# Attention and a spectral feed-forward block on one core: an early table load, two sets of norms for the first pair of heads, and two output tiles that are turned inside the core

## The chip, the core and the metric

The kernel runs on one of the eight cores of a Trainium2 chip. A core has five engines, each with its own instruction stream that runs in order: PE (TensorE, matrix products and transposes), DVE (VectorE), ACT (ScalarE), POOL (GpSimd) and SP (SyncE), which here issues all transfers. Transfers run on 16 DMA engines that all of SP's transfers share. The metric is device time in microseconds of one execution; the kernel before has a median of 2169.73 us over three runs.

## The reference, cut to what matters

```
def rmsnorm(x, g):
    return x / sqrt(mean(x*x, axis=-1) + 1e-6) * g
scores = matmul(rmsnorm(q, g_q), rmsnorm(k, g_k).T) / sqrt(64)
attn = softmax(scores)
x = matmul(attn, v)                      # 8 batches, 12 heads, 448 tokens, 64 each
x = x with heads side by side            # (8, 448, 768)
u = x + real(fft(fft(x, axis=tokens), axis=features))
un = (u - mean(u)) / sqrt(var(u) + 1e-6)
out = u + relu(un @ w_ch1) @ w_ch2       # 768 -> 3072 -> 768
```

All in float32. The two weight matrices come as float64 and are converted inside the kernel.

## The kernel before, in words

Each batch goes through attention, the transform and the feed-forward block. Attention works on pairs of heads, six per batch. For a pair, `load_pair` brings q and k into a tile `raw` (112 partitions; 512 numbers of q and 512 of k on each) and v; `norm_pair` squares them, sums the squares on DVE into `ss` (16 numbers per partition: 8 of q, 8 of k), takes the power -1/2 on POOL and multiplies into `qkn`; PE transposes that (`qk`), ACT and DVE split it into a high and a low part (`QT` of the queries, `KD` and `rounded` of the keys), and then come scores `S`, row minima `mn`, exponentials `P`, transposes `pt` and the product with v. For the first two batches the squares are taken by ACT, later by POOL.

Precision is kept by splitting each operand of the large products in two parts, so every product is made of three passes. A batch's feed-forward block (`ffn`) has 24 steps `up(m)` (18 matmuls each into `h`, line L910 of the profile) and six groups of six steps `down(g, d)` (12 matmuls each into `o`, L931), in the order four `up`, six `down`. The result of `down` is added by DVE to `acc`, which lies transposed: 128 features on partitions, 448 tokens along the row, six such blocks d. Weights come through two streams of three buffers each: one transfer of 768 KB for each `up`, one of 512 KB for each `down`. The transfer for a buffer can be issued when PE has used what it held, so the `w` that step d of `down` uses is asked for when step d-3 has ended.

The 448 tokens of a batch are held in four tiles of 113, 112, 111 and 112 rows. Tiles 0 and 1 hold the even and the odd tokens of the first half *in falling order*, tiles 2 and 3 those of the second half in rising order. `token_tile` makes `u` for a tile, stores it in a DRAM buffer `u_dram` to be used later as the residual, and computes 1/std (`rstd`, the power on POOL). The output of a tile (`output_half`) loads the residual `ur` back, transposes `acc` by PE (`oT`), and DVE forms `ur = oT * rstd + ur`. `store` then writes it out. For tiles 0 and 1, whose rows run backwards, it writes the tile to `u_dram` and issues a second transfer from DRAM to DRAM that reads the rows in reverse, in pieces of 48 numbers (24 where half the columns are stored).

Batch b's feed-forward block runs merged with the attention of batch b+1, and the output of batch b-1 is made in its first four `up` steps. The last batch (7) has no attention beside it; its output is made in two halves of 384 columns (`output_last`), the first after step d=2 and the second after step d=5 of the last group.

Two things set the order. A scheduling step places the instructions of each engine by a model of their times and by the order in which the program writes them, and gives out the buffers of a tag in the order in which the program asks for them; tag `P` has eight buffers, used by `P`, `u`, `un`, `ur` and others. After that each engine, and SP with its transfers, runs strictly in that order: a transfer that waits holds up all that stand behind it.

In the profile nearly all instructions of DVE, ACT and POOL have the line L113, that of a helper which records them, so they are told apart by their tiles.

Of the kernel before, what the change touches and what calls it, by code (L numbers as in the profile page):

```python
# [22 lines left out]
C = 112  # L23
# [66 lines left out]
def spectral_block(ctx, tc, q, k, v, g_q, g_k, w1, w2, d1, d2, out, nb=B):  # L90
# [74 lines left out]
    def add(o, a, b_):  # L165
        V.tensor_tensor(out=o, in0=a, in1=b_, op=ALU.add)
# [18 lines left out]
    u_dram = dram.tile([2, 4, N1, DM], F32, name="u_dram")  # L185
# [679 lines left out]
    residual = {}  # L865

    def output_half(b, i, half, tag):
        n, t0 = LENS[i], OFFS[i]
        if half == 0:
            residual[i] = slot("P", f"ur{b}_{i}")[:, :DM]  # L870
            for r in rows_of(n):
                nc.sync.dma_start(residual[i][r], u_dram[b % 2, i, r])
        u = residual[i]
        op = bank(tag, f"oT{b}_{i}_{half}")
        for j in range(3):
            nc.tensor.transpose(  # L876
                op[:n, j * 128 : (j + 1) * 128],
                accs[b][:, 3 * half + j, t0 : t0 + n],
                ident,
            )  # L880
# [16 lines left out]
    def ffn(b, unT):  # L897
# [27 lines left out]
        def down(g, d):  # L925
# [47 lines left out]

    load_gains()
# [16 lines left out]
    for b in range(nb):  # L991
        merge(
# [25 lines left out]
```

## Time and profile before

| | |
|---|---|
| runs (us) | 2169.73, 2168.72, 2171.92 |
| profiled execution, its own time | 2168.48 us |
| its span, first to last instruction | 2166.7 us |
| PE busy | 2082.8 us, 96% of the span |
| DVE, ACT, POOL busy | 1556.7, 1055.5, 342.6 us |
| mean granted clock of PE | 0.983 |
| moved by DMA | 424.74 MB, mean 196 GB/s |

A row of the timeline gives the start and the length in us, the engine, the line, the operation, the tiles it writes and reads, and in brackets how long the engine was idle ahead of it and what released it. `SPq` is the issue of a transfer on SP. A row of the windows gives a stretch, then for each engine its busy time and (x) its number of instructions, the granted clock of PE, the busy share of the 16 DMA engines and GB/s. Rows of transfers give their number, their size and the median time from issue to landing, where the trace has it.

### The profile page before, as it was taken

The numbers are of one execution on the slowest core, as the hardware profiler recorded it, in microseconds if no ns is written. First come the engines' busy times: TensorE is split into PE (matmuls) and PEld (weight loads), VectorE is DVE, ScalarE is ACT, GpSimd is POOL, SyncE is SP. The second block draws the span as 40 slices with busy tenths as digits, with TensorE's granted clock in tenths as the row PEclk, the third lists the DMA queues.
The fourth block names the chain that finished last, engine by engine and source line by source line (L and its number), as shares of the span: only waits on it lengthen the run. The fifth ranks groups of instructions, "written<-read, shape, count | busy, mean of one in ns | idle before, by whom it ended". The sixth has DMA issues, their size and how long they took to land.

```text
span 2166.7 us, 31325 instructions
## 1 busy us (share of the span) xinstructions
PE 2082.8 (96%) x11224; PEld 1857.7 (86%) x11224; DVE 1556.7 (72%) x3003; ACT 1055.5 (49%) x2258; POOL 342.6 (16%) x196
## 2 busy tenths in 40 slices
PE   7877999899999999999999999999999999999997
PEld 4556777789999999999999999999999999998997
DVE  7888878978785788758786688857787588753122
ACT  7967866455552555435552455425553455422100
POOL 3324434221110111001110111101110011000000
PEclk8988999999999999999999999999999999999999
DMA  5647777677565855667565765658556675449665
GB/s 167 185 131 266 243 262 243 204 236 224 162 174 184 244 173 165 186 200 218 165 174 178 224 194 172 179 183 241 166 173 190 188 219 165 157 157 287 214 211 138
DMA packets 298301, 424.74 MB, mean 196 GB/s; under 512 B 186609, under 2 KB 224482, under 8 KB 298146
## 3 DMA queue, kind: packets, MB, share of 16 engines
q1 hardware_dynamic: 298146, 422.74, 63.8%
q8 instruction: 89, 1.46, 0.3%
q14 instruction: 66, 0.54, 0.1%
HBM read 362.50 MB, written 65.27 MB: 197 GB/s over the span
## 4 chain that ended last, share of the span: by engine, by line
PE 79%; DVE 6%; DMA 6%; ACT 4%; issue 2%; POOL 1%; SPq 0%; DVEq 0%; POOLq 0%; ACTq 0%
PE o L931 29%; PE h L910 28%; PE S L375 6%; PE av L485 4%; DMA dblw<-w 4%; PE pt L473 4%; PE y L590 2%; PE qk L327 1%; DMA w<-w 1%; ACT P L113 1%; PE oT L876 1%; POOL magw L728 1%; PE x L622 1%; DVE qkn L113 1%; PE un L822 1%
## 5 line engine op out<-in xcount | busy, mean ns | idle before, releaser
L931 PE MATMUL o<-hs,w 128*128 128x448 f32 x3456 | 794.8, 372 | 7.0 <-DMA w<-w 2.6
L910 PE MATMUL h<-unT,w 128*128 128x448 f32 x3456 | 778.7, 370 | 4.1 <-ACT unT L113 1.6
L931 PEld LDWEIGHTS o<-hs,w 128*128 128x128 f32 x3456 | 639.5, 189 | 64.5 <-DMA w<-w 4.9
L910 PEld LDWEIGHTS h<-unT,w 128*128 128x128 f32 x3456 | 639.2, 188 | 58.2 <-issue 2.4
L113 ACT ACTIVATE P<-S,mn 112x448 f32<-112x448 f32 x384 | 243.7, 636 | 197.9 <-DVE mn L113 183.9
L113 ACT ACTIVATE hs<-h 128x448 fp32r<-128x448 f32 x192 | 104.3, 543 | 311.6 <-PE h L910 309.7
L113 DVE TENSOR_REDUCE mn<-S 112x1 f32<-112x448 f32 x384 | 233.7, 618 | 28.1 <-PE S L375 25.5
L113 DVE SCALAR_TENSOR_TENSOR hs<-h,hs 128x448 fp32r<-128x448 f32 x192 | 119.4, 622 | 149.2 <-ACT hs L113 147.4
L113 DVE TENSOR_TENSOR acc<-o,acc 128x448 f32<-128x448 f32 x240 | 148.7, 620 | 96.8 <-PE o L931 94.2
L113 POOL TENSOR_TENSOR qkn<-raw 112x1024 f32<-112x1024 f32 x36 | 68.6, 1906 | 697.8 <-PE qk L327 354.8
L113 POOL TENSOR_TENSOR ss<-ss,nhalf 112x16 f32<-112x16 f32 x48 | 144.7, 3014 | 183.2 <-DVE ss L113 164.8
L375 PE MATMUL S<-KD,QT 128*112 128x448 f32 x384 | 152.3, 399 | 16.3 <-ACT KD L113 11.1
L113 ACT CAST T<-pt 128x448 fp32r<-128x448 f32 x216 | 113.1, 533 | 99.8 <-PE pt L473 98.5
L485 PE MATMUL av<-T,vhl 128*128 128x448 f32 x432 | 153.4, 383 | 0.0
L113 DVE TENSOR_TENSOR T<-pt,T 128x448 fp32r<-128x448 f32 x216 | 131.6, 618 | 26.6 <-ACT T L113 25.6
L375 PE MATMUL S<-rounded,QT 128*112 128x448 f32 x384 | 143.2, 375 | 0.4 <-DMA v<-v 0.4
L113 DVE TENSOR_SCALAR P<-P,sm 112x448 f32<-112x448 f32 x288 | 122.5, 463 | 4.1
L473 PE MATMUL pt<-ident,P 112*128 112x112 f32 x864 | 121.8, 259 | 0.0
L473 PEld LDWEIGHTS pt<-ident,P 112*128 112x128 f32 x864 | 102.6, 140 | 15.5
L728 POOL TENSOR_TENSOR magw<-magw,dblw 128x512 uint32<-128x512 uint32 (+1 forms) x46 | 75.4, 1639 | 172.9 <-DVE magw L724 103.1
L113 POOL TENSOR_TENSOR rstd<-st,nhalf 112x1 f32<-112x1 f32 (+2 forms) x32 | 19.6, 612 | 492.3 <-DVE st L113 489.2
L375 PEld LDWEIGHTS S<-KD,QT 128*112 128x112 f32 x384 | 69.2, 181 | 27.9 <-ACT KD L113 13.7
(117 smaller groups left out, 2521.9 us busy)
## 6 DMA issues: line engine op xcount, KB each, us to landing
w<-w SPq DMA_DIRECT2D x192, 768.0 KB, 4.5
w<-w SPq DMA_DIRECT2D x288, 512.0 KB, 4.3
dblw<-w SPq DMA_DIRECT2D x28, 512.0 KB, 5.1
dblw<-w SPq DMA_DIRECT2D x18, 768.0 KB, 5.9
raw<-q SPq DMA_DIRECT2D x96, 112.0 KB, 3.3
raw<-k SPq DMA_DIRECT2D x96, 112.0 KB, 3.7
v<-v SPq DMA_DIRECT2D x96, 96.0 KB, 3.1
u_dram<-u SPq DMA_DIRECT2D x24, 336.0 KB, 3.4
```

What stands on the lines that cost most here:

```text
L113: ins = emit(*args, **kwargs)
L327: nc.tensor.transpose(pt[:, c * C : (c + 1) * C], qk[:, i, c].rearrange("t h d -> t (h d)"), ident[:C, :C],)
L375: ins = nc.tensor.matmul(s_, QT[:, h, cs], K[:, h], start=step == 0, stop=step == 1)
L473: nc.tensor.transpose(pt[:, c * C : (c + 1) * C], Pc[c][:, 512 * h + j * 128 : 512 * h + (j + 1) * 128], ident[:C, :C],)
L485: nc.tensor.matmul(av[:, :S], lv, T[:, i], start=(j == 0 and i == 0), stop=False)
L590: nc.tensor.matmul(o, src[:, par, t0 : t0 + n], D1[:, ri, par, cols], start=i != 1, stop=i != 0,)
L622: nc.tensor.transpose(xp[:n, i * 128 : (i + 1) * 128], src[:, 3 * half + i], ident)
L728: behind(nc.gpsimd.tensor_tensor(out=bits, in0=bits, in1=low, op=ALU.add))
L822: nc.tensor.transpose(pt[:, OFFS[i] : OFFS[i] + LENS[i]], uns[i][:, p * 128 : (p + 1) * 128], ident[: LENS[i], : LENS[i]],)
L876: nc.tensor.transpose(op[:n, j * 128 : (j + 1) * 128], accs[b][:, 3 * half + j, t0 : t0 + n], ident,)
L910: pace(nc.tensor.matmul(o, w[:, a, c], unT[c][:, z], start=n == 0, stop=n == 17))
L931: pace(nc.tensor.matmul(o, w[:, a, f], hs[4 * g + f][:, z], start=n == 0, stop=n == 11))
```

## The change

Three edits.

1. ScalarE's function table is loaded by an instruction of its own at the very start. Before, the load stood directly ahead of ACT's first square and carried that square's waits.
2. For the first pair of the first batch the norms are computed in two passes, q and then k, each with its square, sum, scaling and power, instead of one pass over both.
3. In the last batch tiles 0 and 1 are turned ahead of the store. At the start of that batch's feed-forward block `turn_rstd` copies `rstd` of the two tiles into 32 columns, and reads it and the residual from DRAM back into DRAM in reverse row order. In the last group of `down` the sum is written by two instructions, one for the first 225 tokens in reverse order into a new tile `back` (three feature blocks in one buffer of tag `P`), one for the other 223 into `acc`. The transposes of tiles 0 and 1 read `back`, and the rows come out in rising order, so that `store` writes them to the output directly.

```
-        if b < EARLY:
-            A.activation(sq, flat, AF.Square)
...
-        V.tensor_reduce(ss, sq, axis=AX.X, op=ALU.add)
...
-        G.tensor_tensor(out=ss, in0=ss, in1=nhalf[:C], op=ALU.pow)
+        ss = sb.tile([C, 2, 8], F32, tag="ss", name=f"ss{b}_{p}")
+        for part in ((slice(0, 1), slice(1, 2)) if b + p == 0 else (slice(0, 2),)):
+            n = part.stop - part.start
+            sq = qk[:, part].rearrange("t i c h d -> t (i c h) d")
+            flat = raw[:, part].rearrange("t i h c d -> t (i h c) d")
+            if b < EARLY:
+                A.activation(sq, flat, AF.Square)
...
+            V.tensor_reduce(s_, sq, axis=AX.X, op=ALU.add)
...
+            G.tensor_tensor(out=s_, in0=s_, in1=nhalf[:C, : 8 * n], op=ALU.pow)
@@ def store
-        if i < 2:
+        if i < 2 and b == nb - 1:
+            nc.sync.dma_start(out[b, i : i + 223 : 2, cols], u[n - N2 : n, cols])
+            if i == 0:
+                nc.sync.dma_start(out[b, 224:225, cols], u[:1, cols])
+        elif i < 2:
@@ new
+    def turn_rstd(b):
+        for i in range(2):
+            n = LENS[i]
+            t = sb.tile([N1, 32], F32, tag=f"turned{i}", name=f"turned{b}_{i}", bufs=1)
+            V.tensor_copy(t[:n], rstds[b, i][:n].broadcast_to([n, 32]))
+            nc.sync.dma_start(r_dram[0, i, :n], t[:n])
+            nc.sync.dma_start(
+                r_dram[1, i, :n].rearrange("t (c d) -> c t d", c=16),
+                r_dram[0, i, n - 1 :: -1].rearrange("t (c d) -> c t d", c=16),
+            )
+            nc.sync.dma_start(
+                u_dram[2, i, :n].rearrange("t (c d) -> c t d", c=16),
+                u_dram[b % 2, i, n - 1 :: -1].rearrange("t (c d) -> c t d", c=16),
+            )
+            nc.sync.dma_start(t[:n], r_dram[1, i, :n])
+            turned_rstd[i] = t[:, :1]
@@ def output_half
+                src = u_dram[2 if turn else b % 2, i]
+                nc.sync.dma_start(residual[i][r], src[r])
...
+                back[half][:, j, NT - t0 - n : NT - t0]
+                if turn
+                else accs[b][:, 3 * half + j, t0 : t0 + n],
@@ def down
+            elif b == nb - 1 and g == NG - 1:
+                if d % 3 == 0:
+                    back.append(
+                        slot("P", f"back{d}")[:, : 3 * NT].rearrange(
+                            "r (d t) -> r d t", d=3
+                        )
+                    )
+                add(back[-1][:, d % 3], o[:, NT - 1 :: -1], acc[:, d, NT - 1 :: -1])
+                add(acc[:, d, NT:], o[:, NT:], acc[:, d, NT:])
@@ start
+    nc.scalar.preload_act_table(AF.Exp)
     load_gains()
@@ for b in range(nb)
+        if b == nb - 1:
+            turn_rstd(b)
```

What the scheduling step makes of it, at the places that the prediction speaks of. In these rows the first word is the line, `waits` names the engines and the eight counters of transfers (DMAHW0 to 7) that the instruction waits for.

The start, SP's first transfers, before and then with the change:

```order
L225 DMA raw_0_113<-q 112x4x64 x2
L225 DMA raw_0_113<-k 112x4x64 x2
L190 DMA gains<-g_q 64x1 x2
L190 DMA gains<-g_k 64x1 x2
L225 DMA raw_1_144<-q 112x4x64 [waits DMAHW0_49]
```

```order
L226 DMA raw_0_115<-q 112x4x64 x2
L191 DMA gains<-g_q 64x1 x2
L191 DMA gains<-g_k 64x1 x2
L226 DMA raw_0_115<-k 112x4x64 x2
L226 DMA raw_1_150<-q 112x4x64 [waits DMAHW0_49]
```

The keys' two loads moved behind the four of the gains. And DVE's first instructions there, before and then with the change (`ss` the sums of squares):

```order
L969 MEMSET warm 128x512
L113 TENSOR_REDUCE ss_0_138<-qkn_0_136 112x16 [waits Activation_49]
L113 SCALAR_TENSOR_TENSOR gains<-gains 128x1 [waits DMAHW6_49,DMAHW7_49,DMAHW5_49,DMAHW4_49]
L113 TENSOR_SCALAR ss_0_138<-ss_0_138 112x16 [waits DVE_49]
L113 TENSOR_TENSOR qkn_0_136<-raw_0_113,ss_0_138 112x2x4x64 [waits DMAHW1_49,DMAHW0_49,Pool_49]
L113 TENSOR_TENSOR qkn_0_136<-raw_0_113,ss_0_138 112x2x4x64 [waits DMAHW3_49,DMAHW2_49]
```

```order
L1010 MEMSET warm 128x512
L113 TENSOR_REDUCE ss_0_139<-qkn_0_138 112x8 [waits Activation_49]
L113 TENSOR_SCALAR ss_0_139<-ss_0_139 112x8 [waits DVE_49]
L113 SCALAR_TENSOR_TENSOR gains<-gains 128x1 [waits DMAHW4_49,DMAHW5_49,DMAHW3_49,DMAHW2_49]
L113 TENSOR_TENSOR qkn_0_138<-raw_0_115,ss_0_139 112x2x4x64 [waits DMAHW1_49,DMAHW0_49,Pool_49]
L113 TENSOR_REDUCE ss_0_139<-qkn_0_138 112x8 [waits Activation_49]
L113 TENSOR_SCALAR ss_0_139<-ss_0_139 112x8 [waits DVE_49]
L113 TENSOR_TENSOR qkn_0_138<-raw_0_115,ss_0_139 112x2x4x64 [waits DMAHW7_49,DMAHW6_49,Pool_49]
```

The keys' sum stands behind the queries' product, which waits for POOL. From there to the middle of the first batch's feed-forward block many neighbouring instructions of all engines change places; from the second batch's feed-forward block to the last group of the last batch PE's order is the same.

The border between the feed-forward blocks of batch 6 and batch 7, SP's transfers, before (`u_1`, `u_3` are tiles of batch 7, `ur` residuals of batch 6; `w_249` to `w_251` are for steps d=3 to d=5 of batch 6's last group):

```order
L770 DMA w_170_19821<-w_2_80 128x1536 [waits DMAHW6_49,PE_49]
L635 DMA u_dram<-u_1_19645 112x768 [waits DMAHW7_49,DVE_49]
L770 DMA w_249_19837<-w_5_107 128x1024 [waits DMAHW0_49,PE_49]
L770 DMA w_250_19853<-w_5_107 128x1024 [waits DMAHW1_49,PE_49]
L635 DMA u_dram<-u_3_19667 112x768 [waits DMAHW2_49,DVE_49]
L872 DMA ur_0_19968<-u_dram 112x768 [waits DMAHW3_49,Activation_49]
L872 DMA ur_0_19968<-u_dram 1x768 [waits DMAHW4_49]
L872 DMA ur_1_20008<-u_dram 112x768 [waits DMAHW5_49,Activation_49]
L872 DMA ur_2_20046<-u_dram 96x768 [waits DMAHW6_49]
L770 DMA w_251_19869<-w_5_107 128x1024 [waits DMAHW7_49,PE_49]
```

With the change (the row behind the last is the load of `w_251`):

```order
L883 DMA r_dram<-r_dram 16x113x2 [waits DMAHW6_49]
L773 DMA w_170_19827<-w_2_81 128x1536 [waits PE_49]
L891 DMA turned_0_19925<-r_dram 113x32 [waits DMAHW2_49,DMAHW0_49]
L638 DMA u_dram<-u_1_19651 112x768 [waits DMAHW3_49,DVE_49]
L773 DMA w_249_19843<-w_5_108 128x1024 [waits DMAHW4_49,PE_49]
L887 DMA u_dram<-u_dram 16x112x48 [waits DMAHW5_49,DMAHW3_49]
L773 DMA w_250_19859<-w_5_108 128x1024 [waits PE_49]
L638 DMA u_dram<-u_3_19673 112x768 [waits DMAHW7_49,DVE_49]
L882 DMA r_dram<-turned_1_19931 112x32 [waits DVE_49]
L901 DMA ur_0_19986<-u_dram 112x768 [waits DMAHW1_49,Activation_49]
L901 DMA ur_0_19986<-u_dram 1x768 [waits DMAHW2_49]
L901 DMA ur_1_20026<-u_dram 112x768 [waits Activation_49]
```

The reversing transfers and the waits for their landings stand between the loads of the weights; a first reversing copy and the store of `turned_0` stand ahead of this piece.

The residuals of batch 7 (`ur_0_21124` to `ur_3_21154`) are loaded before the change right behind the border:

```order
L770 DMA w_252_19885<-w_0_102 128x1024 [waits DMAHW2_49,PE_49]
L770 DMA w_253_19901<-w_0_102 128x1024 [waits DMAHW3_49,PE_49]
L872 DMA ur_0_21124<-u_dram 112x768 [waits DMAHW4_49,PE_49]
L872 DMA ur_1_21135<-u_dram 112x768 [waits DMAHW5_49,PE_49]
L872 DMA ur_2_21144<-u_dram 96x768 [waits DMAHW6_49]
L872 DMA ur_0_21124<-u_dram 1x768 [waits DMAHW7_49]
L872 DMA ur_3_21154<-u_dram 112x768 [waits DMAHW0_49,PE_49]
L872 DMA ur_2_21144<-u_dram 15x768 [waits DMAHW1_49]
L770 DMA w_254_19917<-w_0_102 128x1024 [waits DMAHW2_49,PE_49]
```

With the change they are loaded in the last group (`w_284` to `w_287` are the weights of its steps d=2 to d=5):

```order
L773 DMA w_284_21026<-w_5_108 128x1024 [waits DMAHW7_49,DMAHW4_49,PE_49]
L773 DMA w_285_21110<-w_5_108 128x1024 [waits DMAHW5_49,DMAHW0_49,PE_49]
L901 DMA ur_0_21146<-u_dram 112x768 [waits DMAHW1_49]
L901 DMA ur_1_21156<-u_dram 112x768
L901 DMA ur_2_21164<-u_dram 96x768
L901 DMA ur_3_21174<-u_dram 112x768
L773 DMA w_286_21127<-w_5_108 128x1024 [waits DMAHW6_49,PE_49]
L901 DMA ur_0_21146<-u_dram 1x768
L901 DMA ur_2_21164<-u_dram 15x768 [waits DMAHW7_49]
L773 DMA w_287_21144<-w_5_108 128x1024 [waits DMAHW0_49,PE_49]
L855 DMA out_dram<-ur_0_21146 112x384 [waits DMAHW6_49,DMAHW1_49,DVE_49]
L857 DMA out_dram<-ur_0_21146 1x384 [waits DMAHW2_49]
```

All four residuals, 1344 KB, now stand between the weights of d=3 and of d=4: the program asks for a buffer of tag `P` for `back` ahead of those for the residuals, so these are given out behind it.

More of the change, by code (lines that the diff above doesn't have):

```diff
@@ L184, in spectral_block @@
     D2 = rounded[:N1, 2 * S :].rearrange("s (i c a t) -> s i c a t", i=2, c=2, a=2)
-    u_dram = dram.tile([2, 4, N1, DM], F32, name="u_dram")
+    u_dram = dram.tile([3, 4, N1, DM], F32, name="u_dram")
+    r_dram = dram.tile([2, 2, N1, 32], F32, name="r_dram")
     def load_gains():
@@ L249, in norm_pair @@
         qk = sb.tile([C, 2, NC, 2, D], F32, tag="qk", name=f"qkn{b}_{p}", bufs=1)
-        sq = qk.rearrange("t i c h d -> t (i c h) d")
-        flat = raw.rearrange("t i h c d -> t (i h c) d")
-        nth = b * NPAIR + p
-        if b < EARLY:
-            A.activation(sq, flat, AF.Square)
-        else:
-            G.tensor_tensor(out=sq, in0=flat, in1=flat, op=ALU.mult)
-        ss = sb.tile([C, 16], F32, tag="ss", name=f"ss{b}_{p}")
-        V.tensor_reduce(ss, sq, axis=AX.X, op=ALU.add)
-        V.tensor_scalar(
-            out=ss, in0=ss, scalar1=1.0 / D, scalar2=EPS, op0=ALU.mult, op1=ALU.add
-        )
-        G.tensor_tensor(out=ss, in0=ss, in1=nhalf[:C], op=ALU.pow)
+        ss = sb.tile([C, 2, 8], F32, tag="ss", name=f"ss{b}_{p}")
[5 more added lines that the diff above has]
+                A.activation(sq, flat, AF.Square)
+            else:
+                G.tensor_tensor(out=sq, in0=flat, in1=flat, op=ALU.mult)
+            s_ = ss[:, part].rearrange("t i n -> t (i n)")
+            V.tensor_reduce(s_, sq, axis=AX.X, op=ALU.add)
+            V.tensor_scalar(
+                out=s_, in0=s_, scalar1=1.0 / D, scalar2=EPS, op0=ALU.mult, op1=ALU.add
+            )
+            G.tensor_tensor(out=s_, in0=s_, in1=nhalf[:C, : 8 * n], op=ALU.pow)
         for i in range(2):
@@ L266, in norm_pair @@
                 in0=raw[:, i],
-                in1=ss[:, 8 * i : 8 * i + 8]
+                in1=ss[:, i]
                 .rearrange("t (h c) -> t h c", h=2)[:, :, :, None]
@@ L865, in spectral_block @@
     residual = {}
+    turned_rstd = {}
+    back = []
+    def turn_rstd(b):
[14 more added lines that the diff above has]
+            turned_rstd[i] = t[:, :1]
     def output_half(b, i, half, tag):
         n, t0 = LENS[i], OFFS[i]
+        turn = i < 2 and b == nb - 1
         if half == 0:
@@ L871, in output_half @@
             for r in rows_of(n):
-                nc.sync.dma_start(residual[i][r], u_dram[b % 2, i, r])
+                src = u_dram[2 if turn else b % 2, i]
+                nc.sync.dma_start(residual[i][r], src[r])
         u = residual[i]
@@ L882, in output_half @@
         V.scalar_tensor_tensor(
-            out=uh, in0=op[:n, :384], scalar=rstds[b, i][:n], in1=uh,
+            out=uh, in0=op[:n, :384],
+            scalar=(turned_rstd[i] if turn else rstds[b, i])[:n], in1=uh,
             op0=ALU.mult, op1=ALU.add,
```

2 lines of the change are left out of this document (1 added, 1 removed).

## The prediction

> **What bounds the kernel now.** I read the page first (span, busy shares, PE's slices), then a table by stage, then the timeline at the two ends and at the last border between batches, because the change acts only there.
>
> ```profile
> span 2166.7 us, 31325 instructions
> PE 2082.8 (96%) x11224; PEld 1857.7 (86%) x11224; DVE 1556.7 (72%) x3003; ACT 1055.5 (49%) x2258; POOL 342.6 (16%) x196
> PE   7877999899999999999999999999999999999997
> ```
>
> The slices show a kernel that PE bounds from the fifth slice (some 220 us) to the fortieth. Work hidden there costs nothing; what remains is the start, where PE has gaps, and the last slice.
>
> The table by stage (stretch, its length, then PE, PE's weight loads, DVE, ACT, POOL, granted clock, DMA share, GB/s):
>
> ```profile
> 20.00:60.00 40.00, 31.66 (x142) 22.41 (x141) 34.75 (x63) 38.18 (x89) 16.50 (x8) 0.85 0.62 190
> 140.00:180.00 40.00, 25.51 (x120) 21.49 (x121) 31.41 (x63) 24.00 (x48) 10.01 (x7) 0.67 0.36 120
> 1944.00:1954.00 10.00, 10.00 (x56) 9.23 (x55) 5.91 (x17) 5.32 (x11) 1.11 (x2) 1.00 0.65 227
> 1954.00:1964.00 10.00, 10.00 (x61) 9.24 (x60) 3.01 (x9) 3.45 (x5) 0.54 (x1) 1.00 0.81 236
> 1964.00:1974.00 10.00, 8.00 (x46) 7.21 (x45) 5.64 (x11) 2.96 (x8) 0.55 (x1) 1.00 1.03 274
> 1974.00:1984.00 10.00, 10.00 (x56) 9.22 (x56) 3.44 (x6) 1.09 (x2) 0.00 (x0) 1.00 1.03 324
> 2130.00:2140.00 10.00, 10.00 (x51) 9.28 (x50) 2.50 (x4) 1.16 (x3) 0.00 (x0) 1.00 0.01 2
> ```
>
> From 20 to 60 us ACT is the full engine (38.18 of 40), from 140 to 180 none is: a chain of waits bounds there. At 1964 the transfers fill the DMA engines and PE loses 2 us; at 2130 they are idle.
>
> **The start (edits 1 and 2).**
>
> ```profile
> 1.70 1.02 SPq L225 DMA_DIRECT2D raw<-k  x2
> 2.77 1.20 SPq L190 DMA_DIRECT2D gains<-g_q  x2
> 4.01 1.25 SPq L190 DMA_DIRECT2D gains<-g_k  x2
> 5.05 1.28 ACT L113 ACT_TABLE_LOAD   x1 [5.05 <-DMA raw<-k]
> 6.34 1.06 ACT L113 ACTIVATE qkn<-raw 112x1024 f32<-112x1024 f32 x1
> 7.43 1.22 DVE L113 TENSOR_REDUCE ss<-qkn 112x16 f32<-112x1024 f32 x1 [6.04 <-ACT qkn L113]
> 8.69 0.17 DVE L113 TENSOR_SCALAR ss<-ss 112x16 f32<-112x16 f32 x1
> 9.02 2.92 POOL L113 TENSOR_TENSOR ss<-ss,nhalf 112x16 f32<-112x16 f32 x1 [6.91 <-DVE ss L113]
> 11.98 1.29 DVE L113 TENSOR_TENSOR qkn<-raw,ss 112x512 f32<-112x512 f32 x2 [3.11 <-POOL ss L113]
> 12.81 1.11 PE L327 MATMUL qk<-ident,qkn 112*128 112x112 f32 x8 [2.11 <-DVE qkn L113]
> 14.52 0.63 ACT L113 ACTIVATE KD<-qk,gains 64x448 fp32r<-64x448 f32 x1
> 16.73 0.72 PE L375 MATMUL S<-KD,QT 128*112 128x448 f32 x1 [2.80 <-ACT KD L113]
> ...
> L113 POOL TENSOR_TENSOR rstd<-st,nhalf 112x1 f32<-112x1 f32 (+2 forms) x32 | 19.6, 612 | 492.3 <-DVE st L113 489.2 <-DMA ur<-u_dram 3.1
> ```
>
> The first scores (16.73) wait for the first `KD` (14.52). The table load waited for k and took 1.28; it now runs while nothing is there. Keys landed at 5.0, 2.3 after their last issue ended (2.72), so queries land near 4.0 (issue ended 1.66). Then the square of half the size 0.65, the sum 0.65, the scaling 0.3 with its gaps: POOL can start at 5.65. No row has a power of 8 columns; those of 1 (0.61) and 16 (2.92) are its bounds, and on the line between them lies 1.7, which I take: 7.4, the queries' product to 8.05. The keys, behind the gains' 2.45 us of issues, land at 7.5; square to 8.15, sum (DVE free at 8.05) to 8.85, scaling to 9.1, power to 10.85, product 11.55, PE 0.75: `KD` at 12.3 instead of 14.52, 2.2 earlier. ACT, which is full afterwards, gets one instruction more (0.2): **-2.0**. With powers of 2.92 twice the keys come to 14.5 and the gain is 0; with 0.61 it is 3.4. The keys' later load costs nothing, since DVE is held by the queries' product until 8.05; without that cover it would cost 2.45.
>
> Behind this the scheduling step swaps neighbours for some 400 us. The work is the same and ACT stays full, so I take 0; with the idle 14.5 of 40 us in the row of 140 to 180 in mind I allow 3 us either way.
>
> **The border of batch 6 and 7.**
>
> ```profile
> 1953.72 0.32 SPq L635 DMA_DIRECT2D u_dram<-u  x1
> 1955.22 3.11 SPq L770 DMA_DIRECT2D w<-w  x2
> 1961.15 0.34 SPq L770 DMA_DIRECT2D w<-w  x1
> 1969.50 2.72 PE L931 MATMUL o<-hs,w 128*128 128x448 f32 x12 [2.00 <-DMA w<-w]
> ...
> u_dram<-u SPq DMA_DIRECT2D x24, 336.0 KB, 3.4
> u_dram<-u SPq DMA_DIRECT2D x8, 288.0 KB, 2.9
> out_dram<-ur SPq DMA_DIRECT2D x7, 288.0 KB, 6.0
> w<-w SPq DMA_DIRECT2D x288, 512.0 KB, 4.3
> ```
>
> Here the weights come just in time: the last of the group, issued at 1961.15, was used at 1969.50 after a stall of 2.00. The change adds two reversing copies of 336 KB, two reversals of `rstd` in pieces of two numbers, and four small transfers, and SP waits for landings in between. The store of `u_1` (1953.72) now stands behind two such waits, for which I take 2; the weights of d=4 (second issue of the pair at 1955.22, ending 1958.33) then wait for that store's landing (3.4): issue at 1953.7 + 2 + 3.4 + 0.6 = 1959.7 instead of 1958.0. A reversing copy ahead of a transfer cost up to 3.1 (288 KB stored behind one: 6.0 against 2.9), and moves its 336 KB in no less than 1.1 at the 324 GB/s of the full stretch from 1974. I take 2 each. Landing near 1965 against a need at 1964.0, the step is about 1 late; of what reaches the last weights one residual load (288 KB) has moved behind. **+1.3**. Below, 0: the 10 us to 1964 have 1.9 us of unused DMA (share 0.81), the 10 ahead of them 3.5 (0.65). Above, 7: two copies at 3.1 and two reversals that cost the same by piece are 12.4, less these 5.4. ACT's square of `u_3` waits for its store and gets 2 later, with `unT` behind it; the stall at 1969 covers that. DVE's two copies of `rstd` (0.2 each) lie in stretches where DVE is busy 3 to 6 of 10 us. The residuals that no longer load behind 1967 free the engines where PE waited for nothing: no gain.
>
> The Trainium skill, page "DMA: Bandwidth & Descriptors", section Specifications, speaks against this edit: below 512 B a DMA engine reads, modifies and writes. Pieces here have 192 B and 8 B; by that rule the second rival below is the likelier case. No row here prices an 8 B piece.
>
> **The end.**
>
> ```profile
> 2139.24 0.32 SPq L770 DMA_DIRECT2D w<-w  x1
> 2141.68 0.32 SPq L770 DMA_DIRECT2D w<-w  x1
> 2147.59 5.12 PE L931 MATMUL o<-hs,w 128*128 128x448 f32 x24
> 2152.74 0.62 DVE L113 TENSOR_TENSOR acc<-o,acc 128x448 f32<-128x448 f32 x1 [1.81 <-PE o L931]
> 2153.82 2.19 DVE L113 SCALAR_TENSOR_TENSOR ur<-oT,rstd,ur 113x384 f32<-113x384 f32 x4 [0.46 <-PE oT L876]
> 2158.41 0.56 SPq L854 DMA_DIRECT2D out_dram<-u_dram  x1
> 2160.44 1.31 SPq L863 DMA_DIRECT2D out_dram<-ur  x1
> ...
> SPq L1012 <- DMA out_dram<-ur: 3.9, 1, 3.9
> ...
> u_dram<-ur SPq DMA_DIRECT2D x4, 168.0 KB, 2.9
> ```
>
> PE's last product ends at 2152.71, the span at 2166.7: a tail of 14.0, of which DVE needs 3.3 (to 2156.01). The rest is SP: it waits for the writes to `u_dram`, reverses, issues the last store at 2160.44 to 2161.75, and waits 3.9 for it (2165.65); 1.05 follow. With the change: two sums (0.62 splits into about 0.4 and 0.4), transposes behind the first, DVE's four sums start 0.85 behind the product and end at 3.05. Three stores are left to issue, the last starting at 3.9; it lands 2.9 later (6.8), and with 1.05 the tail is 7.85: **-6.15**. A reversed read from PSUM is in no row; at twice the price it adds 0.25.
>
> Against it stand the residuals, now behind the weights of d=3 (2139.24, landing 4.3 later at 2143.5) and ahead of those of d=4. 1344 KB at 274 to 324 GB/s are 4.2 to 5.0, and the 512 KB of d=4 another 1.6 to 1.9: landing at 2149.3 to 2150.4, where PE needs them at 2147.6. The nearest row agrees: at the border a weight behind three such loads and a store came 8.3 after its issue (1961.15 to 1969.50); 2141.68 + 8.3 = 2150.0. Stall **+2.4**; 0 if the idle engines of 2130 to 2140 take it faster, 3.7 with another residual's 1.3 on top. DVE's sums of the first half wait for the last rows of the residuals; d=4 on PE covers them.
>
> Sum: 2168.48 - 2.0 + 1.3 - 6.15 + 2.4 = 2164.0. The execution lies 1.25 under the median of 2169.73 and 0.24 under the fastest run, so I put half of that back: **2164.6**.
>
> **Rivals.**
>
> *The residuals come in time.* For it: DMA share 0.01 before. Against it: the 8.3 above. 2164.6 - 2.4 = 2162.2, chance 0.20.
>
> *The reversals hold SP and the DMA engines at the border (the other side).* Place: between the weights of steps d=3 to d=5 of batch 6; price up to 7; from 5.1 more than my 1.3 nothing of the gain is left. For it: the stall that is there already and share 1.03; against: 5.4 us of free DMA ahead of it, and PE's need at d=4 was met with time. At 7: 2170.3. Chance 0.12.
>
> *The start gives nothing*: two powers of 2.92, or the swapped order loses what the early norms won. 2166.6 to 2169, chance 0.23. By the Trainium skill, "TensorE: Matmul & The Clock Gate", Part 1, an idle window of about 3.4 us halves PE's clock; the clock of 0.67 in the row of 140 to 180 agrees that this stretch has such windows. By it each one more would cost up to 1.7, an estimate from the page's figure, on top of this case.
>
> **How the numbers follow.** The forecast has 0.45. Range 2157.5 to 2170.3: below, the residuals in time, a start of -3.4 and a lucky order; above, the border's 7. A measurement of this kernel tells about 0.2% (4.3 us, below 2165.4) from no change. The forecast is 0.8 inside that, so two thirds of it count as faster (0.30), with all of the first rival (0.20) and little of the third: 0.52. Slower (above 2174.1) needs the border's 7 and a bad order: 0.08. The same: 0.40.
>
> **What would show it.** Right: `KD` first at about 12.3; PE stalled 2 to 3 us on `w` ahead of d=4 of the last group, and 3 to 4 at the border; 8 us from PE's last product of d=5 to the end. Wrong: a tail above 10 us, a stall on `w` at the border above 6, a power of 8 columns near 2.9, or a first score 2 us earlier whose lead is gone by 220 us.

## The result: slower, by 0.68%

| | before | with the change |
|---|---|---|
| median (us) | 2169.25 (four runs) | 2184.03 (four runs, 2182.99 to 2186.51) |
| ratio, 95% interval | | 1.0068 (1.0056 to 1.0081) |
| profiled execution, its time and span | 2168.48, 2166.7 | 2184.48, 2182.6 |

The forecast was 2164.6, 19.4 us below. The milestones of PE in the two traces say where the 15.9 us between the two spans lie:

| stretch (us) | before | change | |
|---|---|---|---|
| start to the first product of batch 1's feed-forward block | 478.5 | 488.2 | +9.7 |
| from there to the first product of batch 6's | 1244.8 | 1245.1 | +0.3 |
| from there to the first product of batch 7's | 249.0 | 258.0 | +9.0 |
| from there to the start of the last product | 180.0 | 183.9 | +3.9 |
| from there to the end | 14.4 | 7.4 | -7.0 |

**The start.** The timeline of the changed kernel, the rows that answer to those of before:

```profile
0.73 1.28 ACT L1015 ACT_TABLE_LOAD   x1 [0.73 <-PEq L1045]
2.15 9.98 PE L1013 MATMUL warmed<-warm,ident 128*128 128x512 f32 x16 [2.15 <-POOL ident masks.py:199]
5.59 1.67 POOL L113 TENSOR_TENSOR ss<-ss,nhalf 112x8 f32<-112x8 f32 x1 [3.49 <-DVE ss L113]
7.29 0.69 DVE L113 TENSOR_TENSOR qkn<-raw,ss 112x512 f32<-112x512 f32 x1 [1.10 <-POOL ss L113]
10.82 0.69 DVE L113 TENSOR_TENSOR qkn<-raw,ss 112x512 f32<-112x512 f32 x1 [1.76 <-POOL ss L113]
11.97 0.93 PE L330 MATMUL qk<-ident,qkn 112*128 112x112 f32 x8
12.56 1.07 ACT L113 CAST QT<-qk 64x448 fp32r<-64x448 f32 x2 [4.43 <-PE qk L330]
13.65 0.63 ACT L113 ACTIVATE KD<-qk,gains 64x448 fp32r<-64x448 f32 x1
15.86 0.46 PE L378 MATMUL S<-KD,QT 128*112 128x448 f32 x1 [2.96 <-ACT KD L113]
```

The power of 8 columns took 1.67, and the keys' product ended at 11.51. But the queries, ready at 7.98, were not transposed until 11.97: the warming products stand ahead of them in PE's order and run to 12.13. So the casts of the queries (12.56) still stand ahead of `KD` on ACT, and the first score comes 0.87 earlier (15.86 against 16.73), not 2.2.

That lead is gone by 40 us: ACT's 24th exponential `P` ends at 39.4 against 38.7 before, its 32nd at 48.2 against 44.8, and PE's 96th product `S` at 120.7 against 111.8. So nearly the whole 9.7 us of the start are lost between 30 and 120 us, and in several waits. One of them, in the timeline of the changed kernel:

```profile
58.84 2.79 SPq L204 DMA_DIRECT2D d2s<-d  x2
65.37 0.57 ACT L113 CAST rounded<-d2s 113x452 fp32r<-113x452 f32 x1 [2.11 <-DMA d2s<-d]
68.43 0.52 ACT L113 COPY T<-pt 128x448 f32<-128x448 f32 x1
69.01 1.55 PE L452 MATMUL av<-T,v 128*128 128x448 f32 x2 [4.29 <-ACT T L113]
```

ACT stands for 2.11 until the transform's table `d2s` has landed, converts it, does four other things, and PE waits 4.29 for the copy `T` behind them. Before, the table's load was issued at 57.08, 1.76 earlier, and ACT did not wait for it. By stretches (length, PE, PE's weight loads, DVE, ACT, POOL, clock, DMA share, GB/s), the changed kernel:

```profile
20.00:60.00 40.00, 29.23 (x127) 18.96 (x128) 34.47 (x59) 35.65 (x82) 15.69 (x8) 0.83 0.55 164
1974.00:1984.00 10.00, 8.28 (x29) 6.85 (x29) 3.22 (x11) 4.14 (x9) 1.08 (x2) 0.66 0.94 255
1984.00:1994.00 10.00, 8.02 (x38) 7.16 (x38) 4.23 (x8) 1.34 (x3) 0.00 (x0) 0.83 0.79 169
```

From 20 to 60 ACT is no longer full: 35.65 of 40 against 38.18. From 60 to 120 it is busy for 52.25, against 58.55 before. That makes 8.8 us of ACT's time lost in 100 us, of the 9.7.

**The border of batch 6 and 7.** SP's issues and PE's long waits in the timeline of the changed kernel, then two rows of SP's waits (in total, times, longest; the longest are those at the border):

```profile
1961.04 0.58 SPq L883 DMA_DIRECT2D r_dram<-r_dram  x1
1961.84 1.72 SPq L773 DMA_DIRECT2D w<-w  x1
1968.64 0.24 SPq L891 DMA_DIRECT2D turned<-r_dram  x1
1968.98 0.87 SPq L638 DMA_DIRECT2D u_dram<-u  x1
1969.94 0.85 SPq L773 DMA_DIRECT2D w<-w  x1
1975.21 4.82 PE L963 MATMUL o<-hs,w 128*128 128x448 f32 x12 [3.76 <-DMA w<-w]
1986.94 4.26 PE L963 MATMUL o<-hs,w 128*128 128x448 f32 x12 [1.98 <-DMA w<-w]
```

```profile
SPq L891 <- DMA r_dram<-r_dram: 7.8, 2, 5.0
SPq L883 <- DMA r_dram<-turned: 2.4, 2, 2.2
```

The reversal of 14 KB of `rstd`, issued at 1961.04, had landed when SP went on at 1968.64, 7.6 later. The store of `u_1` went out at 1968.98 instead of 1953.72 (10.0 of these 15.3 us are the lag with which batch 6 began), the weights behind it at 1969.94, and PE stood for weights at 1975.21, and again at 1986.94. With these two stops its granted clock fell: 0.66 and 0.83 in the stretches from 1974 and from 1984, where before it was 1.00. At full speed the same work would have taken 3.4 and 1.7 us less, as an estimate from these two rows. So the border's 9.0 are about half waiting (the waits for weights sum to 6.1, with a third one of 0.37, against 2.00 before) and about half the lower clock behind them (5.1). What the DMA engines did meanwhile, in 40 slices of 0.5 us from 1956 to 1976 (busy tenths, then GB/s):

```profile
DMA  9999688998997982104548972679999785644039
GB/s 250 224 246 295 240 277 336 315 318 289 436 344 271 147 106 39 1 1 27 38 38 86 74 74 37 135 270 418 345 296 330 203 158 231 256 180 172 25 55 235
```

From 1963.5 to 1968.5 (slices 16 to 25) 1 to 86 GB/s moved. The reversing copy of the residual, in nearly as many pieces but of 192 B, does nothing of the kind in the same trace. The first row below is the stretch behind the first such copy (issued at 1953.55), the second lies behind the reversal of `rstd`, and the third is the landing of the second such copy (issued at 1973.91):

```profile
1957.00:1961.00 4.00, 4.00 (x22) 3.69 (x21) 2.13 (x3) 1.97 (x4) 0.00 (x0) 1.00 0.91 289
1964.00:1968.00 4.00, 4.00 (x25) 3.71 (x24) 2.20 (x7) 0.94 (x1) 0.02 (x1) 1.00 0.54 42
```

```profile
u_dram<-u_dram SPq DMA_DIRECT2D x1, 336.0 KB, 4.4
```

So 1792 pieces of 192 B land in 4.4, and 1808 of 8 B in 7.6. The number of pieces is not what makes the difference.

**The end**, from the timeline and SP's waits of the changed kernel:

```profile
2170.35 2.69 PE L963 MATMUL o<-hs,w 128*128 128x448 f32 x12 [2.20 <-DMA w<-w]
2175.62 0.39 DVE L113 TENSOR_TENSOR back<-o,acc 128x225 f32<-128x225 f32 x1 [1.86 <-PE o L963]
2175.93 0.38 DVE L113 TENSOR_TENSOR acc<-o,acc 128x223 f32<-128x223 f32 x1
2178.72 1.30 SPq L870 DMA_DIRECT2D out_dram<-ur  x3
```

```profile
SPq L1056 <- DMA out_dram<-ur: 1.4, 1, 1.4
```

The stall at d=4 is there (2.20), the reversed sums cost 0.39 and 0.38, the last three stores are issued at 2178.72, SP waits 1.4 for them, and 7.0 us pass between the end of PE's last product (2175.6) and the end, where it was 14.0.

### The profile page after: what moved, and what is told of

Its sections match the earlier page's. It is cut to its first block, busy times and chain, and to the rows that moved or that the text cites. A ratio compares the mean times of both kernels' runs of the same rounds, so it can differ in the third digit from the quotient of the medians.

```text
span 2182.6 us, 31336 instructions
## 1 busy us (share of the span) xinstructions
PE 2090.8 (96%) x11224; PEld 1860.2 (85%) x11224; DVE 1552.0 (71%) x3013; ACT 1056.0 (48%) x2259; POOL 342.4 (16%) x197
## 4 chain that ended last, share of the span: by engine, by line
PE 78%; DMA 7%; ACT 6%; DVE 5%; POOL 2%; issue 2%; SPq 1%; POOLq 0%; DVEq 0%; ACTq 0%
PE h L942 29%; PE o L963 28%; PE S L378 6%; PE av L488 4%; PE pt L476 4%; DMA dblw<-w 3%; DMA w<-w 2%; PE y L593 1%; PE qk L330 1%; ACT P L113 1%; POOL magw L731 1%; PE oT L905 1%; PE x L625 1%; DVE eo L113 1%; PE av L493 1%
## 5 line engine op out<-in xcount | busy, mean ns | idle before, releaser
L963 PE MATMUL o<-hs,w 128*128 128x448 f32 x3456 | 798.1, 373 | 18.1 <-DMA w<-w 10.8
L113 DVE TENSOR_TENSOR acc<-o,acc 128x448 f32<-128x448 f32 (+1 forms) x240 | 147.2, 614 | 86.6 <-PE o L963 83.7
L113 POOL TENSOR_TENSOR ss<-ss,nhalf 112x16 f32<-112x16 f32 (+1 forms) x49 | 143.5, 2929 | 195.9 <-DVE ss L113 165.3
L378 PE MATMUL S<-KD,QT 128*112 128x448 f32 x384 | 152.3, 398 | 12.1 <-ACT KD L113 7.3
```

What stands on the lines that cost most here:

```text
L113: ins = emit(*args, **kwargs)
L378: ins = nc.tensor.matmul(s_, QT[:, h, cs], K[:, h], start=step == 0, stop=step == 1)
L963: pace(nc.tensor.matmul(o, w[:, a, f], hs[4 * g + f][:, z], start=n == 0, stop=n == 11))
```

## The experiments

Two theories at the outset. *Order and pieces*: the 9.7 us come from the order in which the scheduling step puts the neighbours after edit 2, and the 9.0 from the reversal of `rstd` in pieces of 8 B. The rivals: the table load or the two passes themselves cost the start; SP's chain of waits costs the border, whatever the pieces; the edits influence each other. The kernel before, run beside these, had medians of 2168.3 to 2169.9 and single runs from 2164.4 to 2175.1, and a profiled execution lay up to 9 us beside its kernel's median; so ratios with their intervals decide. The last four columns are the milestones of each kernel's profile, the stretches of the table above without the second.

| kernel | median | ratio (95%) | batch 1 starts | 6 to 7 | in 7 | tail |
|---|---|---|---|---|---|---|
| edit 1 alone | 2168.3 | 0.9993 (0.9983 to 1.0003) | 475.5 | 249.0 | 179.1 | 14.4 |
| edit 2 alone | 2177.86 | 1.0042 (1.0026 to 1.0057) | 486.8 | 251.5 | 179.5 | 14.5 |
| edit 2, old order | 2170.53 | 1.0010 (0.9999 to 1.0020) | 477.0 | 251.2 | 180.4 | 14.6 |
| no edit, new order | 2180.54 | 1.0053 (1.0034 to 1.0071) | 489.1 | 251.6 | 179.9 | 14.1 |
| edit 2, old order of loads | 2179.56 | 1.0039 (1.0029 to 1.0050) | 483.7 | 250.9 | 179.8 | 14.1 |
| edit 3 alone | 2178.09 | 1.0039 (1.0024 to 1.0053) | 480.3 | 259.6 | 185.8 | 7.4 |
| edit 3, wide pieces | 2169.05 | 0.9996 (0.9983 to 1.0008) | 476.9 | 253.2 | 189.2 | 7.3 |
| whole change, wide pieces | 2176.56 | 1.0038 (1.0025 to 1.0051) | 488.1 | 253.0 | 184.1 | 7.5 |
| edit 3, turned late | 2174.72 | 1.0031 (1.0019 to 1.0043) | 480.0 | 252.7 | 195.1 | 7.5 |
| the same, residuals early | 2177.1 | 1.0038 (1.0026 to 1.0050) | 483.0 | 253.2 | 189.0 | 7.6 |
| the same with edit 1 | 2178.19 | 1.0040 (1.0028 to 1.0053) | 478.1 | 253.1 | 191.6 | 7.6 |
| the same, wide pieces | 2169.02 | 0.9990 (0.9981 to 0.9999) | 476.5 | 252.4 | 185.4 | 7.5 |
| turned at the border, wide, residuals early, edit 1 | 2166.42 | 0.9983 (0.9973 to 0.9994) | 477.9 | 251.7 | 182.9 | 7.6 |
| the same, residuals spread | 2169.19 | 1.0003 (0.9991 to 1.0016) | 477.6 | 252.2 | 184.4 | 7.6 |

### The start: which edit, and is it the work or the order

Edit 1 alone is one line:

```
+    nc.scalar.preload_act_table(AF.Exp)
     load_gains()
```

> Edit 1 alone: the function table loaded at the start, everything else as before (every engine's order is then the same as before). In the changed kernel the first 480 us cost 9.9 us more than before. Theory (order): that loss belongs to the new order that edit 2 sets off, so this kernel stays within 1.5 us of the kernel before (2167.7 to 2170.7), with a first score some 1 us earlier at most, because POOL's power of 16 columns (2.92) still stands behind the landing of the keys. Rival (table): the early load itself disturbs the start, and about 10 us are lost here: 2179.

Measured 0.9993: the early table costs nothing that could be told and gives at most 0.17%. In its timeline the first score comes at

```profile
15.69 0.46 PE L375 MATMUL S<-KD,QT 128*112 128x448 f32 x1 [2.81 <-ACT KD L113]
```

1.04 earlier, with POOL's power of 16 columns left as it was. (In all kernels with edit 1, edit 2 or both the first score comes between 15.24 and 15.96; the two do not add up.) Edit 2 alone (`norm_pair` of the change in the kernel before):

> Edit 2 alone: the first pair's norms in two passes, q and then k, and with it the new order of neighbours up to the middle of the first batch's feed-forward block; no early table load, no edit 3. Theory (order): the whole loss of the first 480 us is here, 2179 +- 2, with batch 1's feed-forward block starting near 488 instead of 478.5. Rival (table): the two passes are harmless and this kernel is at 2167 to 2170.

Measured 1.0042, 8.0 us, with batch 1 at 486.8. Its timeline has the stop at 65 us too:

```profile
64.36 0.57 ACT L113 CAST rounded<-d2s 113x452 fp32r<-113x452 f32 x1 [1.66 <-DMA d2s<-d]
67.99 1.86 PE L451 MATMUL av<-T,v 128*128 128x448 f32 x2 [3.82 <-ACT T L113]
```

Then the same edit with the order held. The table `ISSUE` lists, for each engine, the instructions in the order of the kernel before:

```
+    for engine, text in ISSUE.items():
+        ...
+        for one, two in zip(rows, rows[1:]):
+            tc.add_manual_dep(mine[two], mine[one].name,
+                DependencyInfo(NoSync, DATA), reason="issue order")
```

> Edit 2 alone, with the order of every engine behind the first pair's norms held to that of the kernel before (PE's first 1793 instructions, DVE's 642, ACT's 556, SP's 300, POOL's 90), so that only the two passes themselves and the first loads differ. Theory (order): the loss is gone, 2166 to 2170. Rival (work): the two passes themselves, with one ACT instruction, two DVE and one POOL instruction more, cost it, and this kernel stands beside edit 2 alone at 2177 to 2181.

Measured 1.0010 (0.2 us faster to 4.3 slower): with the old order 7.3 of the 8.0 us are gone. The reverse, the kernel before with the new order and not one instruction changed:

> None of the three edits: the kernel before, its instructions unchanged, with the order of every engine held to the one that edit 2 sets off (PE's first 1793 instructions, DVE's 642, ACT's 556, SP's 300, POOL's 90). Theory (order): it loses what edit 2 alone lost, 8 +- 2: 2177.5. Rival (the loss needs the two passes together with the new order): within 2 us of the kernel before.

Measured 1.0053, 12 us, more than the 8 +- 2 expected; but its interval overlaps that of edit 2 alone, so the two cannot be told apart. Nothing but the order of the first quarter was new, and the stop at 66 us is in its timeline as well:

```profile
66.41 0.57 ACT L211 CAST rounded<-d2s 113x452 fp32r<-113x452 f32 x1 [2.00 <-DMA d2s<-d]
70.04 1.31 PE L547 MATMUL av<-T,v 128*128 128x448 f32 x2 [4.17 <-ACT T L211]
```

ACT's time tells which kernels lose and where. Two rows of the stretches, the kernel before and then its instructions in the new order, and the waits of ACT from 20 to 120 us in the same two (in total, times, longest; one row of before, three of the other):

```profile
60.00:120.00 60.00, 49.82 (x255) 32.31 (x254) 55.21 (x95) 58.55 (x129) 24.38 (x14) 1.00 0.54 152
60.00:120.00 60.00, 48.94 (x224) 32.40 (x224) 48.06 (x87) 53.05 (x119) 20.52 (x10) 0.91 0.55 165
```

```profile
ACT P L113 <- DVE mn L113: 0.6, 2, 0.5
ACT P L211 <- DVE mn L211: 4.8, 8, 2.0
ACT rounded L211 <- DMA d2s<-d: 2.0, 1, 2.0
ACT w1e L827 <- POOL magw1e L826: 1.5, 1, 1.5
```

| kernel | ACT busy, 20 to 60 | 60 to 120 | idle in the 100 us | batch 1 starts |
|---|---|---|---|---|
| before | 38.18 | 58.55 | 3.3 | 478.5 |
| edit 1 alone | 38.02 | 58.52 | 3.5 | 475.5 |
| edit 2, old order | 37.70 | 58.53 | 3.8 | 477.0 |
| the whole change | 35.65 | 52.25 | 12.1 | 488.2 |
| edit 2 alone | 35.54 | 52.69 | 11.8 | 486.8 |
| no edit, new order | 35.49 | 53.05 | 11.5 | 489.1 |

The three kernels with the new order have ACT idle 8 to 9 us longer there than the kernel before, the two others do not. The waits are the same in the three: some 5 us for DVE's row minima `mn` in eight waits, 1.7 to 2.1 for the table `d2s`, 2.1 for two steps of POOL on the weights. So the order is the cause, shown from both sides, and it costs through many small waits of ACT. Is one of them, the late load of the table, most of it? In the next kernel only SP's order is held:

```
+        if engine not in ('SP',):
+            continue
```

> Edit 2 alone, with only SP's first 300 transfers held to the order of the kernel before; the other engines are ordered by the scheduling step as it likes. In the changed kernel ACT waits 2.11 us at 65 us for the transform's table, whose load stands later in SP's order, and PE 4.29 behind it. Theory (one late load): with the transfers in the old order most of the loss is gone, 2170 to 2173. Rival (the order of the engines as a whole): no single load is the cause, and this kernel is still at 2175 or above; PE's and ACT's order differs from that of both other kernels here.

Measured 1.0039: the theory of the one load falls. Batch 0's feed-forward block does begin early there (175.9, against 178.5 before and 184.3 with edit 2 alone), so up to that point the order of the loads cost; but then 7.8 us are lost inside that block, where the engines' order is a third one. Between 178 and 488 us PE waits there 6.3 us for ACT's part of the weights `w` and 7.0 for ACT's copies `T`, against 1.5 and 3.4 before. That the order of SP alone does not give the time back is shown; what each single row of the order costs stays open.

### The border: pieces, or SP's chain

Edit 3 alone, with the start of before:

> Edit 3 alone: turning rstd and the residual at the border of batch 6 and 7, reversed sums and the direct stores at the end; the start as before, in the order of before. The traces of before and after give +8.8 at the border, +4 within batch 7 (2.2 of it the stall on the weights of d=4) and -7.0 behind the last product. Theory (the three edits add up): 2169.3 + 5.8 = 2175 +- 1.5. Rival (the loss at the border depends on what the new start shifts ahead of it): within 2 us of before or below.

Measured 1.0039, 8.2 us: the edits add up (0.42% and 0.39% alone, less 0.07% for edit 1, against 0.68% together, all within the intervals). Two of its stretches, in the columns of the table by stage, and the wait in its timeline:

```profile
1956.00:1960.00 4.00, 3.92 (x23) 3.44 (x21) 2.58 (x9) 0.95 (x2) 0.40 (x1) 1.00 0.80 40
1960.00:1964.00 4.00, 3.83 (x25) 3.35 (x23) 0.00 (x0) 0.00 (x0) 0.00 (x0) 1.00 0.70 54
```

```profile
1970.60 4.13 PE L961 MATMUL o<-hs,w 128*128 128x448 f32 x12 [6.76 <-DMA w<-w]
```

Behind the reversal (issued at 1955.44) the DMA engines are busy for 0.70 to 0.80 of the time and move 40 to 54 GB/s, against 324 in the full stretch of before. If SP's waiting for landings were all, it would leave them idle. But SP does wait as well: 7.4 us, from 1957.05 to 1964.47, for the landing of this reversal. The test changes the pieces alone:

```
-                r_dram[1, i, :n].rearrange("t (c d) -> c t d", c=16),
-                r_dram[0, i, n - 1 :: -1].rearrange("t (c d) -> c t d", c=16),
+                r_dram[1, i, :n].rearrange("t (c d) -> c t d", c=2),
+                r_dram[0, i, n - 1 :: -1].rearrange("t (c d) -> c t d", c=2),
```

> Edit 3 alone, with one difference: the two reversals of rstd in DRAM go in 2 x 113 pieces of 64 B instead of 16 x 113 pieces of 8 B (the same 14 KB). In the trace of edit 3 alone the moved rate falls to 33 to 45 GB/s for some 8 us right behind the issue of the first of these reversals at 1955.44, with the DMA engines busy, and PE then waits 6.76 us for weights. Theory (pieces): the number of pieces is the price; with an eighth of them the weights come through, the loss at the border (10.6 us from the start of batch 6 to that of batch 7) falls to 3 +- 3 and the time to 2171 +- 2. Rival (SP's chain): what costs is that SP waits for one landing after the other ahead of the weights, whatever the pieces; the loss stays at 8 to 11 and the time at 2176 to 2180.

Measured 0.9996: 9 us came off, with the same transfers in SP's chain, so the rival in its form "whatever the pieces" falls. From its timeline:

```profile
1952.55 0.66 SPq L881 DMA_DIRECT2D r_dram<-r_dram  x1
1955.73 0.24 SPq L889 DMA_DIRECT2D turned<-r_dram  x1
1973.00 4.26 PE L961 MATMUL o<-hs,w 128*128 128x448 f32 x12 [2.00 <-DMA w<-w]
```

The next step on SP goes 3.2 behind the issue, where it was 9.0 (1955.44 to 1964.47) with pieces of 8 B; SP's wait for the landing is 1.5 instead of 7.4. So the small pieces can cost in two ways, by holding SP and by slowing the weights that are already under way, and this pair alone does not part them. The profiled execution of the kernel with wide pieces lies 6.7 us above the median, so its columns do not show all of the gain: the border fell from 259.6 to 253.2, but batch 7 took 189.2, with a clock of 0.67 from 2004 to 2014 behind a stall of 2.93. The same in the whole change:

> The whole change with one difference: rstd is reversed in 2 x 113 pieces of 64 B instead of 16 x 113 of 8 B. The whole change has a ratio of 1.0068 (1.0056 to 1.0081) to the kernel before. Theory (pieces and order are two separate losses): the 9 us that wide pieces gave to edit 3 alone (2178.1 to 2169.05) come off here as well, 2169.5 + 14.8 - 9 = 2175 +- 2. Rival (with the new start the border is late anyway): 2180 or above.

Measured 1.0038: 6.5 us less than the whole change by the ratios (0.0030), of the 9 expected; the 1.0038 that remains is about what edit 2 alone costs (1.0042). Moving the turning away from the border is the other way to spare the weights; each step is issued behind a weight load of batch 7 and held there:

```
+    TURN = {(1, 0): (turn_a, 0), (1, 1): (turn_a, 1), (1, 4): (turn_b, 0),
+            (2, 1): (turn_b, 1), (2, 4): (turn_c, 0), (3, 1): (turn_c, 1)}
...
+                if b == nb - 1 and (g, d) in TURN:
+                    step, i = TURN[g, d]
+                    step(b, i)
                 down(g, d)
```

> Edit 3 alone, with the turning moved: the copies, reversals and loads of rstd and the reversal of the residual are issued one after the other behind weight loads of the groups 1 to 3 of batch 7's feed-forward block, where the weights are early, not at the border. Theory: the border loss is gone (batch 7 starts within 2.5 us of the kernel before), the stall at d=4 of the last group stays (2.1 to 2.2), the tail stays 7 shorter: 2169.9 - 7 + 4 = 2167 +- 2. Rival (the reversals cost wherever they stand): the loss moves with them into batch 7 as stalls on weights of 4 us or more, 2172 or above.

The rival held, at 1.0031. Its timeline, and the weights among its transfers from 2060 to 2080:

```profile
2064.45 1.11 SPq L890 DMA_DIRECT2D r_dram<-r_dram  x1
2076.77 7.67 PE L975 MATMUL o<-hs,w 128*128 128x448 f32 x24 [5.99 <-DMA w<-w]
```

```profile
w<-w SPq DMA_DIRECT2D x4, 512.0 KB, 10.8
```

In the middle of a steady group PE stops for 5.99 behind the reversal (x1, 14 KB), and weights land 10.8 behind their issue, against 4.3 over the kernel before. SP waits for no reversal here: the weights that PE stops for were issued at 2065.93, right behind it, and landed at 2076.72. So the second way costs by itself. The reversing copy of the residual was issued 0.6 us ahead of the reversal, though, so which of the two slows the weights is open up to here; the kernel with wide pieces below settles it.

### The residuals, and a version that beats both

```
+                if b == nb - 1 and g == 4 and d < 4:
+                    load_residual(b, d)
                 down(g, d)
```

> As the kernel with the turning moved, and the four residuals of batch 7 are asked for and loaded one by one behind weight loads of group 4, ahead of the buffers for the reversed sums, instead of all between the weights of d=3 and d=4 of the last group. Theory: the stall of 2.2 at d=4 goes and nothing takes its place: 2 to 3 below the kernel with the turning moved alone, 2164.5 +- 2. Rival (1344 KB cost PE the same wherever they are loaded): same time as with the turning moved alone.

The stall at d=4 is gone from the trace (in the kernel with the turning late it was 2.79), but the time did not fall: 1.0038 against 1.0031, intervals that overlap. A step of 2 us under the stop of 6 at 2078 can't be told here. With edit 1 on top:

> As the kernel with turning and residuals moved, with edit 1 (early table load) on top, which leaves the order as it was; edit 2 left out. Edit 1 alone gave a ratio of 0.9993 (0.9983 to 1.0003). Theory: tail -7.0, start -1, border and last group 0: 2162 +- 2, a ratio of 0.9963. Rival: the tail's gain is eaten by new waits in batch 7 and the ratio stays above 0.998.

A miss, 1.0040, for the same 6 us. Then the pieces widened in it:

> Edits 1 and 3 with the turning issued late (groups 1 to 3 of batch 7), the residuals loaded one by one in group 4, and the reversals of rstd in 2 x 113 pieces of 64 B. With the 8 B pieces the same order had a stall of 6.2 us behind the first reversals, at 2074 to 2078. Theory (pieces): that stall goes, no other comes; the tail's 7 us and the early table's 1 remain: 2162 +- 3, ratio 0.9965. Rival (the reversing of the residual, 678 KB in pieces of 192 B, is what held the weights there): a stall of 3 us or more stays at the same place, ratio 0.999 or above.

Measured 0.9990, a gain of 9 by the medians (11 by the ratios), as in edit 3 alone, but 5 us short of the theory. Where the stop of 6.2 was there is

```profile
2067.21 5.15 PE L982 MATMUL o<-hs,w 128*128 128x448 f32 x24 [1.45 <-DMA w<-w]
```

so the pieces of 8 B were its cause and the reversing of the residual, which is unchanged, at most the rest. They cost wherever they stand. The turning left at the border, with wide pieces and early residuals:

> Edits 1 and 3 with the turning left where the change puts it, at the border of batch 6 and 7, but with pieces of 64 B for rstd, and the residuals loaded one by one in group 4. Theory: beside the kernel with wide pieces alone (0.9996) the stall of 2.4 at d=4 goes: 2166 +- 2. Rival (the place matters as much as the pieces): the border loses 4 us or more against the kernel that turns late, and this one stays at 2168 or above. If both are equal, the place is of no weight once the pieces are wide.

Measured 0.9983 (0.9973 to 0.9994), 2166.42, as the theory had it: the lowest of all, and below the kernel before by 0.17% (0.06 to 0.27). Its interval overlaps that of the kernel that turns late (0.9990), so with wide pieces the place is of no weight that could be told, and that of edit 1 alone (0.9993). Its largest stall in batch 7 is

```profile
2121.64 2.71 PE L975 MATMUL o<-hs,w 128*128 128x448 f32 x12 [1.19 <-DMA w<-w]
```

and to take that away the loads were spread over four groups (`g in (1, 2, 3, 4) and d == 3`):

> As the kernel with the turning at the border in wide pieces (ratio 0.9983), but the four residuals are loaded one in each of the groups 1 to 4, behind the weights of step d=3, instead of all in group 4, where a stall of 1.19 was left at 2121. Theory: that stall goes, 1 to 1.5 us less: 2165 +- 1.5, ratio 0.9976. Rival (the loads are hidden already and the 1.19 was chance): ratio 0.9983 +- 0.0005.

Measured 1.0003: both theories missed. The trace has three stalls of 1.02 to 1.80 in batch 7, among them

```profile
2130.29 2.72 PE L975 MATMUL o<-hs,w 128*128 128x448 f32 x12 [1.40 <-DMA w<-w]
```

and the intervals of the two hardly touch, so spreading does not help and may hurt; why, stays open.

## Why the prediction was wrong, step by step

- **What bounds the kernel.** Right as far as PE goes; "ACT stays full" behind the start was the reason for taking the new order at 0, and it did not stay full (35.65 of 40 and 52.25 of 60, against 38.18 and 58.55).
- **The start, -2.0.** The chain was well worked out as far as DVE: the power of 8 columns 1.67 (taken 1.7), the keys' product at 11.51 (taken 11.55). The term was mis-sized behind it: `KD` came at 13.65, not 12.3, since PE's warming products to 12.13 were left out, and with them the queries' transposes and the 1.07 of their casts ahead of `KD`. Worth 0.87 instead of 2.2.
- **The new order, 0 +- 3.** This is the step that failed first. Edit 2 with its order costs 8.0 (1.0042), the order alone 12 (1.0053), against 0.7 with the old order held. "The work is the same and ACT stays full" left out that the neighbours now come in an order in which ACT waits: 8 to 9 us more idle time from 20 to 120 us in each kernel with the new order. The warning was in the quoted profile: an ACT at 38.18 of 40 has no room for a neighbour that comes first and waits. "A lead that is gone by 220 us" was named as a sign of error; it was gone by 40.
- **The border, +1.3 (0 to 7).** The step that failed second: 9.0, outside its own bounds. The two waits of SP that it took at 2 together were 2.2 and 5.0, and the slower clock behind PE's stops, 5.1, was in no term. The mechanism was named as a rival with chance 0.12; its upper price (two reversals at 3.1) took the reversal of 14 KB to cost no more than a reversing copy of 336 KB in as many pieces, which is where it failed: the copy landed in 4.4 and left the rate behind it at 289 GB/s, the reversal took 7.6 with 8 B pieces (9.0 in edit 3 alone), with 42 GB/s, and 3.2 or less in an eighth of the pieces of 64 B. The sign of error named for it, a stall above 6, did not show (3.76), since half of the loss is clock. The Trainium skill's rule ("DMA: Bandwidth & Descriptors", Specifications: below 512 B a DMA engine reads, modifies and writes) pointed the right way: the prediction itself called this rival the likelier case by it, and still gave it 0.12. But pieces of 64 B and of 192 B are below 512 B too and cost little, so the rule alone does not give the size of it.
- **The stall at d=4, +2.4.** Right: 2.20, so the rival with the residuals in time falls. The batch lost 3.9 in all; 1.36 more is a wait for weights at 2020.79, behind the late border, which the prediction did not have.
- **The end, -6.15.** Right, a little small: 7.0. A reversed read from PSUM has no price (0.39 and 0.38 for the halves of 0.62).
- **The sum.** Of the 20.5 us between the sum (2164.0) and the profiled execution (2184.48), the start with the new order has 11.7, the border 7.7, batch 7 1.5, the batches between 0.3, less 0.85 at the end. The tail and the stall came out as worked; the two terms without a row of their own, the order and the 8 B piece, were taken near zero.

## What to carry to other kernels

An order that a scheduling step chose is part of what is measured: where an edit moves neighbours on a full engine, hold the old order and time the edit apart, for here the order cost 8 to 12 us and the edit itself nothing that could be told. Look for very small pieces in a reversal inside DRAM, not at its bytes or at their number: 14 KB in 1808 pieces of 8 B kept SP from its next step for 7.6 to 9.0 us at the border and stopped PE for 6 in the middle of a steady group, where 336 KB in 1792 pieces of 192 B landed in 4.4 and 14 KB in 226 pieces of 64 B cost 9 us less. Price a stop of PE with the clock behind it: at the border that was as much again as the waiting. A saving in the tail is only worth what its preparation does not cost in a stretch where weights come just in time.

## What was not expected of the hardware

A transfer in 1808 pieces of 8 B slows all others: around it and behind it 1 to 86 GB/s moved, with the DMA engines busy for half of the time, and weights of 512 KB landed in 10.8 instead of 4.3. The time is not in the pieces themselves. The packet records of the changed kernel's trace give each 8 B piece 9 ns (15 ns for one of 192 B), and 1259 of the 1808 had started by 1963.5. What takes long are the weights' packets: the 30 of 6144 B that started from 1965.0 to 1968.5 took 1.1 us on average, where the median before is 0.23. Whether it is the 8 B as such or that sixteen pieces share a row of 128 B, and what holds the other packets, no run here shows.

The 16 warming products, the same in all kernels, took 8.55 to 10.08 us. In the trace's record of the clock full speed was granted from 5.05 us before and from 7.92 with the change; if PE ran at half speed until then, the 2.87 us between are worth 1.43, just the difference between 8.55 and 9.98. The Trainium skill, "TensorE: Matmul & The Clock Gate", Part 1, says that the ramp of the clock differs from run to run; the traces agree. Here it set when the first transposes could begin.
